# Five instruction orders searched anew, with token parts ahead of raw weights and scatters led by their own copies

## The chip, the cores and the metric

The kernel runs on one core of a Trainium2 chip. Its engines work side by side, each through its own list of instructions: TensorE (PE) multiplies, VectorE (DVE) and ScalarE (ACT) work element by element, GpSimd (POOL) copies and issues indirect DMAs, SyncE (SP) issues the other DMAs. The metric is the device time of one execution in microseconds, the median of several runs.

## The reference

A gated linear recurrence over four sequences of 5056 tokens with 256 channels, and then a mixture of eight experts that sends each token to one expert:

```python
log_a = 8.0 * sigmoid(r_gate) * log(clip(sigmoid(a_param), 1e-6, 1 - 1e-6))
a_t = exp(log_a)
x_gated = sqrt(maximum(1 - a_t * a_t, 1e-6)) * sigmoid(i_gate) * x
h = a_t[:, t] * h + x_gated[:, t]         # for every t; y[:, t] = h
logits = y @ w_gate                        # (20224, 8)
e = argmax(logits, axis=1); gate = softmax(logits)[e]
out[token] = gate * (maximum(y[token] @ w1[e], 0) @ w2[e])    # w1: 256x1024, w2: 1024x256
```

## The kernel before

Tokens are cut into 158 blocks of 128, four blocks to a quad (40 quads, the last one shorter). The front works quad by quad: three loads (r, i, x; `load`, L638), tanh and exp on ScalarE (`th` L647, `ex` L653, `ti` L658), square and square root (`sq` L669, `rt` L675), a product on VectorE (`b` L680) and the recurrence as a scan along the tokens (`scan` L699). TensorE then computes gate logits (`lp` L718, `lt` L733, copied by `ls` and `lg`) and turns the rows token-major (`yt` L756). VectorE takes each row's largest absolute value (`am` L763, `sc`), ScalarE writes the row scaled to float16 (`hi` L783) and VectorE the rest that float16 left over (`lw` L793).

Quads form groups (`GROUPS`). For each group `r1` to `r6` find the expert and the place of every token, with one product on TensorE between (`rk` L830), and the factor `mx`. POOL writes token id and factor behind each row (L786, L879 for the first four quads; L881, L882 for the others, four blocks at once) and scatters the rows block by block into a DRAM buffer sorted by expert (`scat` L888). A fence on SP (`fence` L933) waits for a group's scatters.

The experts work in slots of 256 rows (the last 16 of 128): first layer (`L1` L1129), relu on ScalarE (L1141) and its rest on VectorE (L1149), second layer (`L2` L1169 to L1173), scaled copy out of PSUM (`ot` L1182), and a scatter into the output (`store` L1193). Slots 0 to 7 take the raw float32 weights of experts 0 to 7 (`raw` L1042), one slot each; meanwhile those weights are split into two float16 parts and written back (`wm` L975/L977, `wt` L981, `wh` L995, `wl` L1000, `wr` L1004). Later slots load the split weights (`w` L1057), by a table (`tab`, L1209 on) that says which rows and which expert a slot has.

The first `PICK` = 2 slots don't wait for the buffer: `sel` (L910) makes a 0/1 matrix of the tokens that belong to them, `pick` (L922) multiplies the token rows by it, and `xs` (L928) copies the columns from PSUM, which the first layer then reads. Slots 2 to 7 load their rows from the buffer transposed (`xl` L1080, L1087), and `join` (L1100) adds the two float16 halves on POOL.

The order on every engine comes from a planner that runs before the kernel is built: a list scheduler (`Line`, `Plan`) with a duration, a priority and buffer pools for each task. Priorities are a due time per quad or slot plus an offset per kind (`URGE`). The instructions are then written out in that order and each engine works through its list in order, so an instruction that waits holds up everything behind it on its engine.

## Time and profile before

| | us |
|---|---|
| median of 3 runs (lowest to highest) | 1052.61 (1051.04 to 1054.34) |
| profiled execution | 1058.75 |
| its span, first to last instruction | 1057.0 |
| ScalarE's idle time before its first instruction and before its first data | 0.74 and 0.62 |
| TensorE busy / VectorE / ScalarE / POOL | 989.3 / 676.3 / 619.1 / 435.9 |

The profile comes from one execution, some 6 us above the median. The mean granted TensorE clock is 0.988 of full speed. A window view gives busy time per engine in a stretch; a timeline row gives start, duration, engine, line, operation and tiles, and in square brackets how long the engine sat idle before it and what ended that.

### The profile page before, as it was taken

Reading aid. Unit: us, or ns where it says so; the run is one execution under the profiler, and the core shown is the slowest. Engines: PE = TensorE matmul, PEld = TensorE weight load, DVE = VectorE, ACT = ScalarE, POOL = GpSimd, SP = SyncE. Lnnn points to the kernel's source line nnn. Section 1 sums busy time; section 2 is a strip of 40 time slices with the busy share of each in tenths; the row PEclk is TensorE's granted clock in tenths of the full one; section 3 lists DMA queues with packets and bytes.
Section 4 is the critical chain, followed back from the end, with each engine's and each line's share of the span. In section 5 each row is a group of like instructions: output and inputs, shape, how many; then the busy total and the mean of one; then the engine's idle time right before and its main releaser. Section 6 shows DMA issues by size and latency. Waiting matters only on the chain. (4 is left out here: it accounts for less than half of the span.)

```text
span 1057.0 us, 23781 instructions
## 1 busy us (share of the span) xinstructions
PE 989.3 (94%) x8854; PEld 862.1 (82%) x8854; DVE 676.3 (64%) x1387; ACT 619.1 (59%) x815; POOL 435.9 (41%) x522
## 2 busy tenths in 40 slices
PE   1469899999999999999999999999999999999997
PEld 1138688888888989888888888888888888889987
DVE  4998889887686565876847578466876473232211
ACT  8988685675746467567555765557666442222222
POOL 0264446434555335363452644525264434222222
...
GB/s 367 382 248 209 329 339 314 291 328 369 333 299 290 344 246 342 275 379 203 286 343 356 271 310 269 297 329 302 235 321 295 310 321 140 262 265 326 223 249 26
DMA packets 169347, 307.12 MB, mean 291 GB/s; under 512 B 117636, under 2 KB 122377, under 8 KB 147978
## 3 DMA queue, kind: packets, MB, share of 16 engines
q1 hardware_dynamic: 153770, 262.81, 78.4%
...
## 5 line engine op out<-in xcount | busy, mean ns | idle before, releaser
L1129 PE MATMUL p<-xT,wt 128*128 128x256 f16 (+1 forms) x3936 | 413.6, 263 | 2.5 <-DMA wt<-wscr 2.2
L1129 PEld LDWEIGHTS <-wt 128*128 128x128 f16 x3936 | 354.9, 98 | 40.8 <-DMA wt<-wscr 2.5
L1193 POOL DMA_INDIRECT out<-ot,meta x164 | 181.1, 1104 | 400.2 <-ACT ot L1182 353.7
L1171 PE MATMUL po<-wt,hb 128*128 128x256 f16 x1184 | 322.9, 273 | 8.3 <-ACT ot L1182 6.4
L1149 DVE SCALAR_TENSOR_TENSOR hb<-p,hb 128x1024 f16<-128x1024 f32 x148 | 180.5, 1220 | 224.3 <-ACT hb L1141 207.2
L1173 PE MATMUL po<-wt,hb 128*128 128x256 f16 x1184 | 322.8, 273 | 0.1
L1172 PE MATMUL po<-wt,hb 128*128 128x256 f16 x1184 | 322.8, 273 | 0.1
L1141 ACT ACTIVATE hb<-p 128x1024 f16<-128x1024 f32 (+1 forms) x164 | 167.4, 1021 | 196.7 <-PE p L1129 167.8
L888 POOL DMA_INDIRECT buf<-rows,pi x158 | 172.4, 1091 | 47.8 <-issue 35.8
L1182 ACT ACTIVATE ot<-po,f 128x256 f32<-128x256 f32 x148 | 69.9, 472 | 172.7 <-PE po L1173 125.3
L1172 PEld LDWEIGHTS <-hb 128*128 128x128 f16 x1184 | 115.8, 98 | 21.7 <-issue 8.7
L1171 PEld LDWEIGHTS <-hb 128*128 128x128 f16 x1184 | 115.8, 98 | 16.6 <-issue 2.7
L1173 PEld LDWEIGHTS <-hb 128*128 128x128 f16 x1184 | 115.8, 98 | 13.7 <-issue 0.3
L699 DVE TENSOR_TENSOR_SCAN in_x<-in_r,in_x 128x512 f32<-128x512 f32 (+7 forms) x82 | 97.5, 1198 | 1.4
L680 DVE SCALAR_TENSOR_TENSOR in_x<-in_i,in_x 128x1024 f32<-128x1024 f32 (+1 forms) x38 | 45.7, 1203 | 48.8 <-ACT in_i L675 40.8
L1112 POOL TENSOR_SCALAR f<-meta,wt,wt 128x2 f32<-128x2 f32 (+1 forms) x82 | 37.5, 458 | 95.5 <-DMA wt<-wscr 76.6
L793 DVE SCALAR_TENSOR_TENSOR rows<-yt,fa,rows 128x256 f16<-128x256 f32 x154 | 65.4, 478 | 14.1 <-ACT rows L783 7.1
L783 ACT ACTIVATE rows<-yt,fa 128x256 f16<-128x256 f32 x154 | 61.8, 475 | 7.2 <-DVE fa L775 6.2
L1169 PE MATMUL po<-wt,hb 128*128 128x256 f32 x256 | 62.1, 392 | 1.5 <-ACT ot L1180 1.3
L664 DVE SCALAR_TENSOR_TENSOR in_x<-in_i,in_x 128x1024 f32<-128x1024 f32 (+1 forms) x38 | 46.2, 1221 | 23.5 <-ACT in_i L658 18.5
L1129 PE MATMUL p<-x,wt 128*128 128x256 f32 x256 | 59.3, 386 | 0.7 <-ACT x L928 0.7
L763 DVE TENSOR_REDUCE m<-yt 128x2 f32<-128x512 f32 x77 | 50.2, 678 | 11.2 <-PE yt L756 10.8
...
## 6 DMA issues: line engine op xcount, KB each, us to landing
wt<-wscr SPq DMA_DIRECT2D x164, 1024.5 KB
...
out<-ot,meta POOLq DMA_INDIRECT x164
```

The lines of the kernel that those rows point to most:

```text
L699: V.tensor_tensor_scan(y[:, lo:hi], av[:, lo:hi], y[:, lo:hi], init, ALU.mult, ALU.add)
L793: V.scalar_tensor_tensor(r[:, 2 * p + j, D:2 * D], o["yt", p][:, j], o["sc"][:, 2 * p + j:2 * p + j + 1], r[:, 2 * p + j, 0:D], ALU.mult, ...
L888: i = G.indirect_dma_start(out=buf[:, :], out_offset=bass.IndirectOffsetOnAxis(ap=g["pi"][:, b0 + j:b0 + j + 1], axis=0), in_=rows[q]["row ...
L1129: T.matmul(pv[:, i], wv[:, wl, kk, fs], o["xT"][:, 2 * xl + kk, 0:U], start=(z == 0), stop=(z == len(seq) - 1))
L1141: A.activation(o["h"][:, gs, 0:U] if o["raw"] else o["h"][:, 0, gs, 0:U], o["p1", g], AF.Relu)
L1149: V.scalar_tensor_tensor(o["h"][:, 1, gs, 0:U], o["p1", g], 0.0, o["h"][:, 0, gs, 0:U], ALU.max, ALU.subtract)
L1169: T.matmul(dst, h[:, f, ts], wv[:, f, :], start=(f == 0), stop=(f == NF - 1))
L1171: T.matmul(dst, h[:, 0, f, ts], wv[:, 0, f, :], start=(f == 0), stop=False)
L1172: T.matmul(dst, h[:, 0, f, ts], wv[:, 1, f, :], start=False, stop=False)
L1173: T.matmul(dst, h[:, 1, f, ts], wv[:, 0, f, :], start=False, stop=(f == NF - 1))
L1182: A.activation(o["ot", j], o["po", j], AF.Copy, scale=o["f2"][:, j:j + 1])
L1193: i = G.indirect_dma_start(out=out[:, :], out_offset=bass.IndirectOffsetOnAxis(ap=o["id"][j], axis=0), in_=o["ot", j], in_offset=None, bou ...
```

## The change

The planner gets new durations and group sizes, a priority offset for nearly every single task (the table `NUDGE`, about 1500 entries; one line of it is shown), and a model of how many DMAs may be under way. One slot is picked instead of two. For the first 15 quads (`ROWSUM`) the row's measure is the sum of absolute values, taken on ScalarE by an activation with an accumulator, in place of the largest absolute value on VectorE. The sum of the two halves for raw slots (`join`) moves from POOL to VectorE. For quads that aren't picked, `scat` copies id and factor of its own block before the scatter. The two weight sums under way may use two PSUM columns.

```diff
-GROUPS = (2, 2, 2, 2, 1, 2, 3, 2, 1, 2, 2)
+GROUPS = (1, 3, 2, 2, 1, 2, 1, 2, 1, 1, 2)
 UNITS = 4
-SINGLE = 6
+SINGLE = 2
 BATCH = 2
 PASSES = ((1, 256, 8),)
...
-PICK = 2
-EARLY = 250.0
-ELOAD = 90.0
+PICK = 1
+ROWSUM = 15
+ADDER = 'DVE'
+EARLY = 622.8
+ELOAD = 748
 WIDE = (3,)
...
-URGE = dict(quad=23.0, load=-22.0, norm=-37.0, rows=-11.5, hi=197.0, route=-208.0, scat=335.0, tab=-203.0,
-            first=-850.0, slot=-3250.0, fac=-52.0, store=-90.0)
+URGE = dict(quad=25.2, load=-137.0, norm=-105.3, rows=-55.5, hi=1053.8, route=-211.5, scat=1126.0, tab=-1395.2, first=-482.8, slot=-3722.3, fac=-106.7, store=399.0)
+NUDGE = {
+"L1(0,0)": -59.2, "L1(0,1)": -20, "L1(1,0)": -4, "L1(1,1)": -347.3, "L1(10,0)": 228.2, "L1(10,1)": 2.7,
...
-BUFS = dict(r=3, i=4, x=6, rows=4, yt=2, lp=1, rank=1, tot=1, lg=4, hl=2, xT=4, hb=3, ot=9, po=1, p1=2, reg=3, x32=6)
+BUFS = dict(r=3, i=4, x=6, rows=4, yt=2, lp=1, rank=1, tot=2, inc=4, lg=4, hl=2, xT=4, hb=3, ot=9, po=1, p1=2, reg=3, x32=6)
...
+    LANES = 8
+    DMAS = dict(load=1, raw=1, wr=1, w=1, fence=1, xl=2, blank=2, pads=E)
...
+            if q < ROWSUM:
+                T["am", q, p] = a("ACT", 0.78, pr + URGE["rows"], "am", q, p, after=[T["yt", q, p], T.get(("am", q, 0))], take=[("rows", q)] if p == 0 else [])
+            else:
+                T["am", q, p] = a("DVE", 0.64, pr + URGE["rows"], "am", q, p, after=[T["yt", q, p]])
...
-            T["fa", q] = a("POOL", 0.5, pr + URGE["scat"], "fa", q, after=[T["r6", c], T["hi", q, 0], T.get(("fence", c - 1))] + list(xs),
-                           give=[("lg", c)])
+            if s.picked(q):
+                T["tag", q] = a("POOL", 0.75, pr + URGE["scat"], "tag", q, after=[T["hi", q, 0]])
+            ok = [T["r6", c], T["hi", q, 0], T.get(("fence", c - 1)), T.get(("tag", q))] + list(xs)
+            if s.picked(q):
+                T["fa", q] = a("POOL", 0.65, pr + URGE["scat"], "fa", q, after=ok, give=[("lg", c)])
+                ok = [T["fa", q]]
             for j in range(s.quads[q]):
-                sc.append(a("POOL", 1.27, pr + URGE["scat"], "scat", q, j, after=[T["fa", q], T["lw", q, j // 2]], give=[("rows", q)],
-                            size=0.45))
+                sc.append(a("POOL", 1.28 if s.picked(q) else 1.9, pr + URGE["scat"], "scat", q, j, after=ok + [T["lw", q, j // 2]],
+                            give=[("rows", q)] + ([] if s.picked(q) else [("lg", c)]), size=0.4))
         if g[-1] == s.nq - 1:
             sc = [a("SP", 3.0, -500, "pads", c, after=sc, size=6.0)]
-        T["fence", c] = a("SP", 0.4, -500, "fence", c, after=sc, then=lambda t: s.routed(c))
...
+    def fenced(s, c):
+        s.routed(c)
+        s.add("DVE", 0.01, -1e6, "drop", c, after=[s.tabbed], give=[("inc", c)])
...
-            x = a("POOL", 1.2 * U / 256 + 0.1, -160, "join", k, after=[x], take=[("x32", k)], give=[("xT", k)])
+            if ADDER == "PE":
+                x = T["add", k] = a("PE", 0.5, -98, "add", k, after=[x], take=[("yt", ("x", k))], give=[("xT", k)], slack=SLACK)
+                x = a("ACT", 0.5, -205, "join", k, after=[x], take=[("x32", k)], give=[("yt", ("x", k))])
+            elif ADDER == "DVE":
+                x = a("DVE", 0.1 + 0.5 * U / 256, -205, "join", k, after=[x], take=[("x32", k)], give=[("xT", k)])
+            else:
+                x = a("POOL", 1.2 * U / 256 + 0.1, -160, "join", k, after=[x], take=[("x32", k)], give=[("xT", k)])
...
+    def token_rows(o):
+        if "rows" not in o:
+            o["rows"] = work.tile([P, QB, PITCH], F32, name="rows", bufs=BUFS["rows"])
+        return o["rows"]
+
     @op
     def am(q, p):
         o = rows[q]
-        if p == 0:
+        if "m" not in o:
             o["m"] = small.tile([P, QB], F32, name="m", bufs=4)
-        V.tensor_reduce(o["m"][:, 2 * p:2 * p + 2], o["yt", p], AX.X, ALU.max, apply_absolute_value=True)
+        if q < ROWSUM:
+            r = token_rows(o).bitcast(BF16)
+            for j in range(2 * p, 2 * p + 2):
+                A.activation(r[:, j, 0:D], o["yt", p][:, j % 2], AF.Abs, accum_out=o["m"][:, j:j + 1])
+        else:
+            V.tensor_reduce(o["m"][:, 2 * p:2 * p + 2], o["yt", p], AX.X, ALU.max, apply_absolute_value=True)
 
...
     @op
     def hi(q, p):
         o, nb = rows[q], plan.quads[q]
-        if p == 0:
-            o["rows"] = work.tile([P, QB, PITCH], F32, name="rows", bufs=BUFS["rows"])
+        r = token_rows(o).bitcast(F16)
         for j in range(2):
-            A.activation(o["rows"].bitcast(F16)[:, 2 * p + j, 0:D], o["yt", p][:, j], AF.Copy, scale=o["sc"][:, 2 * p + j:2 * p + j + 1])
-        if p == 0 and plan.group_of[q] <= PASSES[0][0]:
-            for j in range(nb):
-                G.tensor_copy(o["rows"].bitcast(I32)[:, j, D + 1:PITCH], ids[:, q * QB + j:q * QB + j + 1].to_broadcast([P, PITCH - D - 1]))
+            A.activation(r[:, 2 * p + j, 0:D], o["yt", p][:, j], AF.Copy, scale=o["sc"][:, 2 * p + j:2 * p + j + 1])
 
     @op
...
+    def mark(q, j):
+        G.tensor_copy(rows[q]["rows"].bitcast(I32)[:, j, D + 1:PITCH], ids[:, q * QB + j:q * QB + j + 1].to_broadcast([P, PITCH - D - 1]))
+
     @op
     def fa(q):
         g, b0, _ = group(q)
-        r, nb = rows[q]["rows"], plan.quads[q]
-        if plan.group_of[q] <= PASSES[0][0]:
-            for j in range(nb):
-                G.tensor_copy(r[:, j, D:D + 1], g["mx"][:, b0 + j:b0 + j + 1])
-            return
-        G.tensor_copy(r.bitcast(I32)[:, 0:nb, D + 1:PITCH], ids[:, q * QB:q * QB + nb].unsqueeze(2).to_broadcast([P, nb, PITCH - D - 1]))
-        G.tensor_copy(r[:, 0:nb, D:D + 1], g["mx"][:, b0:b0 + nb].unsqueeze(2))
+        for j in range(plan.quads[q]):
+            G.tensor_copy(rows[q]["rows"][:, j, D:D + 1], g["mx"][:, b0 + j:b0 + j + 1])
+
+    @op
+    def tag(q):
+        for j in range(plan.quads[q]):
+            mark(q, j)
 
     @op
     def scat(q, j):
         g, b0, _ = group(q)
         c = plan.group_of[q]
+        if not plan.picked(q):
+            mark(q, j)
+            G.tensor_copy(rows[q]["rows"][:, j, D:D + 1], g["mx"][:, b0 + j:b0 + j + 1])
         i = G.indirect_dma_start(
             out=buf[:, :], out_offset=bass.IndirectOffsetOnAxis(ap=g["pi"][:, b0 + j:b0 + j + 1], axis=0),
             in_=rows[q]["rows"][:, j, :], in_offset=None, bounds_check=E * plan.cap - 1, oob_is_err=False)
...
-            g["sel"] = work.tile([P, 2, NF, 256], F16, name="hb", bufs=BUFS["hb"]).rearrange("p l f u -> p (l f u)")[:, 0:B * PICK * 256]
+            g["sel"] = work.tile([P, 2, NF, 256], F16, name="hb", bufs=BUFS["hb"]).rearrange("p l f u -> p (l f u)")[:, 0:B * PICK * PASSES[0][1]]
...
-                    T.matmul(st["pick"][:, h, 0:PICK * 256], r[:, j, l * D + h * P:l * D + (h + 1) * P], g["sel"][:, b0 + j].rearrange("p k u -> p (k u)"),
+                    T.matmul(st["pick"][:, h, 0:PICK * PASSES[0][1]], r[:, j, l * D + h * P:l * D + (h + 1) * P], g["sel"][:, b0 + j].rearrange("p k u -> p (k u)"),
...
     def join(k):
 
         o = slots[k]
-        U = o["U"]
         x = work.tile([P, 2, 256], F32, name="x32", bufs=BUFS["x32"])
-        G.tensor_tensor(x[:, :, 0:U], o["xT"][:, 0:2, 0:U], o["xT"][:, 2:4, 0:U], ALU.add)
+        if ADDER == "PE":
+            A.copy(x, o["xT"])
+        else:
+            U = o["U"]
+            (V if ADDER == "DVE" else G).tensor_tensor(x[:, :, 0:U], o["xT"][:, 0:2, 0:U], o["xT"][:, 2:4, 0:U], ALU.add)
         o["xT"] = x
...
     def wt(e, i):
-        T.matmul(misc[:, 508:509], ones32, prepared[e, i]["m"], start=True, stop=True)
+        o = prepared[e, i]
+        staged(o)
+        z = 508 + next(sums) % BUFS["tot"]
+        o["tot"] = misc[:, z:z + 1]
```

Three places of the written order follow, the first on SP: the start of the queue of loads, behind the loads of constants. `in_r`, `in_i`, `in_x` and `hb` are tiles for the gates and tokens of a quad, `wt` tiles for raw weights, 1 MB each (a load of 128x1024 is 0.52 MB). Before:

```order
L1042 DMA wt12_141<-in_w 128x2048
L1042 DMA wt02_138<-in_w 128x2048
L638 DMA in_r_147<-in_rix 128x1024
L638 DMA in_i_149<-in_rix 128x1024
L638 DMA in_x_151<-in_rix 128x1024
L1042 DMA wt11_140<-in_w 128x2048
L1042 DMA wt01_137<-in_w 128x2048
L1042 DMA wt10_139<-in_w 128x2048
L1042 DMA wt00_136<-in_w 128x2048
L638 DMA hb_158<-in_rix 128x1024 x2
L638 DMA in_x_162<-in_rix 128x1024
L638 DMA hb_165<-in_rix 128x1024 x2
```

And now (`hb_95` has gates of the third quad, `hb_155` of the fourth; `buf_80` is the buffer, which is filled with padding rows):

```order
L1134 DMA in_i_149<-in_rix 128x1024
L1134 DMA in_x_151<-in_rix 128x1024
L1134 DMA in_i_153<-in_rix 128x1024
L1134 DMA hb_155<-in_rix 128x1024
L1134 DMA in_x_157<-in_rix 128x1024
L1134 DMA hb_155<-in_rix 128x1024
L1134 DMA in_r_164<-in_rix 128x1024
L1560 DMA wt00_138<-in_w 128x2048
L1134 DMA hb_95<-in_rix 128x1024
L1560 DMA wt01_139<-in_w 128x2048
L1831 DMA buf_80<-pad_129 256x1x272 x2
L1134 DMA in_x_186<-in_rix 128x1024
```

Six raw weights stood ahead of the token parts (`in_x_162`, later `in_x_168`) of the third and fourth quad; now two raw weights are queued by the time that all four quads have their parts, the last at `in_x_186`.

The second place is ScalarE's queue in front of the copy `xs` (`x32_678` before, `x32_641` now), which hands the picked columns to slot 0. L975 and L1485 are `wm`, L995 and L1509 `wh`, L783 and L1288 `hi`, L675 and L1171 `rt`. The 12 rows that end with it, before:

```order
L975 ACTIVATE hl_553,wm_552<-wt11_140 128x2048
L849 ACTIVATE lg_495<-lg_495 128x64
L653 ACTIVATE in_r_231<-in_r_231,k4_89 128x1024
L975 ACTIVATE hl_573,wm_572<-wt01_137 128x2048
L669 ACTIVATE in_i_190<-in_r_231 128x1024
L675 ACT_TABLE_LOAD
L675 ACTIVATE in_i_185<-in_i_185,quarter_103 128x1024
L995 ACTIVATE hl_553<-wt11_140,wsc_631 128x2048
L675 ACTIVATE in_i_190<-in_i_190,quarter_103 128x1024
L658 ACT_TABLE_LOAD
L658 ACTIVATE in_i_204<-in_i_204 128x1024
L928 COPY x32_678<-p1_383 128x512
```

Now, rows of the new order that end 11 ahead of that copy (L1267 is the new row reduction `am`):

```order
L1509 ACTIVATE hl_348<-wt01_139,wsc_389 128x2048
L1485 ACTIVATE hl_411,wm_410<-wt00_138 128x2048
L1267 ACTIVATE rows_435,m_434<-yt_404 128x256 x2
L1221 COPY ls_441<-misc_133 128x128
L1267 ACTIVATE rows_435,m_434<-yt_429 128x256 x2
L1267 ACTIVATE rows_457,m_456<-p1_443 128x256 x4
L1288 ACTIVATE rows_435<-yt_404,fa_350 128x256 x2
L1351 ACTIVATE lg_315<-lg_315 128x96
L1288 ACTIVATE rows_435<-yt_429,fa_350 128x256 x2
L1149 ACTIVATE in_r_164<-in_r_164,k4_89 128x1024
L1288 ACTIVATE rows_457<-p1_443,fa_350 128x256 x4
L1154 ACTIVATE in_i_265<-in_i_265 128x1024
```

Before, two of the four sums of weights (L975) and one of the three scaled parts (L995) stood directly ahead of the copy, with two table loads. Now row reductions (L1267) stand between the sums of weights and the row copies (L1288), and of the sums of weights only two are left ahead of the copy.

The third place is POOL, from the last picked quads on: L879 and L1382 copy factors, L786 and L1376 ids, L888 and L1397 scatter, L1100 is the sum `join`, L1188 and L1717 scale, L1193 and L1722 store. Before (rows of the last two picked quads, `rows_506` and `rows_519`):

```order
L879 COPY rows_506<-mx_545 128x1 x4
L888 DMA buf_80<-rows_506,pi_568 166400x272 x4
L879 COPY rows_519<-mx_545 128x1 x4
L888 DMA buf_80<-rows_519,pi_568 166400x272 x4
L1100 ISA
L1100 TENSOR_TENSOR x32_799<-xT_742 128x512
L1100 TENSOR_TENSOR x32_821<-xT_757 128x512
L1100 TENSOR_TENSOR x32_852<-xT_777 128x512
L1188 TENSOR_SCALAR ot_854<-ot_854,meta_733 128x256
L1100 TENSOR_TENSOR x32_862<-xT_784 128x512
L1193 DMA out_0<-ot_854,meta_733 20224x256
```

And now, without the numbers of the tiles:

```order
L1376 COPY rows<-ids 128x15 x8
L1382 COPY rows<-mx 128x1 x12
L1397 DMA buf<-rows,pi 166400x272 x12
L1722 DMA out<-ot,meta 20224x256
L1717 ISA
L1717 TENSOR_SCALAR ot<-ot,meta 128x256 x2
L1722 DMA out<-ot,meta 20224x256 x3
L1376 COPY rows<-ids 128x15
L1396 COPY rows<-mx 128x1
L1397 DMA buf<-rows,pi 166400x272
```

The sums of two halves are gone from POOL. The factors of the last three picked quads stand together in front of their 12 scatters, which slot 1 now waits for. From the fourth group on, each scatter has its own copy of id and factor in front, where one pair of copies (L881, L882) led four scatters.

## Rows read from the trace of the kernel before

**Rows 1.** The page: busy time, share and instructions of each engine.

```profile
PE 989.3 (94%) x8854; PEld 862.1 (82%) x8854; DVE 676.3 (64%) x1387; ACT 619.1 (59%) x815; POOL 435.9 (41%) x522
```

**Rows 2.** Windows: start:end, length; busy time (x count) of PE, PEld, DVE, ACT, POOL; PEclk; DMA share; GB/s.

```profile
0.00:79.79 79.79, 32.97 (x176) 16.57 (x176) 61.18 (x153) 71.38 (x84) 26.41 (x49) 0.91 0.89 334
10.00:30.00 20.00, 4.49 (x29) 3.19 (x29) 10.94 (x20) 19.12 (x22) 0.92 (x5) 1.00 1.01 418
80.42:104.35 23.93, 23.93 (x130) 20.38 (x131) 20.77 (x33) 22.00 (x24) 10.13 (x9) 1.00 0.74 197
104.35:131.30 26.95, 22.84 (x111) 17.94 (x110) 22.35 (x25) 17.23 (x20) 12.64 (x10) 0.91 1.04 324
131.30:1052.30 921.00, 909.53 (x8441) 807.18 (x8439) 571.37 (x1179) 507.34 (x686) 385.13 (x455) 1.00 0.92 290
```

**Rows 3.** Groups by line, ACT, 0 to 79.79: count, busy us, mean ns, idle before.

```profile
L975 ACT ACTIVATE hl<-wt 128x2048 bf16<-128x2048 f32 x4 | 7.6, 1909 | 0.0
L675 ACT ACT_TABLE_LOAD x5 | 6.4, 1283 | 0.1
L995 ACT ACTIVATE hl<-wt,wsc 128x2048 f16<-128x2048 f32 x3 | 5.9, 1987 | 0.0
...
L975 ACT ACTIVATION_READ_ACCUMULATOR hl<-wt 128x1 f32 x4 | 0.8, 201 | 0.0
```

**Rows 4.** Timeline of ACT: start us, duration us, engine, line; [idle before, releaser].

```profile
21.55 1.56 ACT L783 ACTIVATE rows<-yt,fa 128x256 f16<-128x256 f32 x4
...
79.79 1.07 ACT L928 COPY x<-p 128x512 f32<-128x512 f32 x2 [0.89 <-PE p L922]
```

**Rows 5.** Timeline of PE around the first slots and at slot 8.

```profile
80.42 3.72 PE L1129 MATMUL p<-x,wt 128*128 128x256 f32 x16 [0.67 <-ACT x L928]
...
88.40 1.07 PE L718 MATMUL misc<-in_x,wg 128*32 128x256 f32 x16
...
92.96 0.38 PE L733 MATMUL misc<-cst,ls 128*128 128x128 f32 x2
93.18 0.28 PE L981 MATMUL misc<-wm,ones 128*128 128x1 f32 x2
93.32 3.70 PE L1169 MATMUL po<-wt,hb 128*128 128x256 f32 x16
96.86 0.60 PE L756 MATMUL yt<-cst,in_x 128*128 128x128 f32 x4
...
205.14 2.78 PE L1129 MATMUL p<-xT,wt 128*128 128x256 f16 x24
```

**Rows 6.** Timeline of POOL: scatters, first sum, the fourth group.

```profile
51.65 2.80 POOL L879 COPY rows<-mx 128x1 f32<-128x1 f32 x4
...
69.40 0.72 POOL L879 COPY rows<-mx 128x1 f32<-128x1 f32 x4 [6.91 <-DVE mx L871]
...
75.69 3.91 POOL L879 COPY rows<-mx 128x1 f32<-128x1 f32 x4
...
84.58 0.97 POOL L888 DMA_INDIRECT buf<-rows,pi  x1 [0.30 <-issue]
96.06 1.16 POOL L1100 TENSOR_TENSOR x<-xT 128x512 f32<-128x512 f16 x1 [10.51 <-DMA xT<-buf]
...
143.99 0.98 POOL L1193 DMA_INDIRECT out<-ot,meta  x1 [10.84 <-DMA in_i<-in_rix]
```

**Rows 7.** L879 by itself: min, median, max in ns.

```profile
L879 POOL COPY rows<-mx x16: 176/258/2246, 45.3 to 78.4; 128x1 f32<-128x1 f32 x16
```

**Rows 8.** Groups by line, POOL, whole span.

```profile
L879 POOL COPY rows<-mx 128x1 f32<-128x1 f32 x16 | 8.1, 555 | 41.2 <-DVE mx L871 41.2
...
L786 POOL COPY rows<-ids 128x15 int32<-128x15 int32 x16 | 4.5, 326 | 8.2 <-DMA ids<-in_ids 8.2
```

**Rows 9.** Timeline of SP's queue: the fences at L933.

```profile
90.84 0.25 SPq L933 DMA_DIRECT2D fence<-buf  x1
...
183.42 0.26 SPq L933 DMA_DIRECT2D fence<-buf  x1
```

More of the change, by code (lines that the diff above doesn't have):

```diff
@@ L180, in run @@
                         continue
+                    if e == "POOL" and k.size and now < s.clear(e) - 1e-9:
+                        continue
                     p = (k.prio + (SWITCH if k.table and k.table != s.act else 0), k.seq)
@@ L206, in run @@
                     k.end = s.dma + 1.2
+                    if k.name == "xl" and k.size > 1:
+                        d = max(d, s.dma - 0.5 - now)
+                        s.free[e] = now + d
+                        heappush(s.events, (now + d, next(s.ids), None))
                 else:
                     k.end = now + d
+                n = 1 if e == "POOL" and k.size else 0 if e != "SP" else 1 if k.name == "xl" and k.args[0] < PICK else s.DMAS.get(k.name, 0)
+                if n:
+                    s.lanes[e] += [k.end if k.size else now + 2.0] * n
+                    z = s.clear(e)
+                    if z > now + d:
+                        if e == "SP":
+                            s.free[e] = z
+                        heappush(s.events, (z, next(s.ids), None))
                 heappush(s.events, (k.end, next(s.ids), k))
@@ L370, in route @@
+        T["r3", c] = a("DVE", 0.58 * f, pr, "r3", c, after=[T["rk", c]], take=[("inc", c)], give=[("rank", c)])
+        T["r4", c] = a("DVE", 0.2 * f, pr, "r4", c, after=[T["r3", c]])
+        T["gt", c] = a("ACT", 0.2 * f, pr - 6, "gt", c, after=[T["r1", c]], table="T")
+        T["r5", c] = a("DVE", (0.45 if c <= PASSES[0][0] else 0.3) * f, pr, "r5", c, after=[T["r4", c]])
+        T["r6", c] = a("DVE", 0.7 * f, pr, "r6", c, after=[T["gt", c], T["r5", c]] + [T["sc", q] for q in g])
         sc = []
@@ L481, in slot @@
         assert not near or raw
-        x = T["xl", k] = a("SP", 0.5 if near else 1.7, p0 + (0.3 if head else 0.1), "xl", k, after=[reg], take=[] if near else [("xT", k)], give=gr,
+        x = T["xl", k] = a("SP", 0.5 if near else 1.95, p0 + (0.3 if head else 0.1), "xl", k, after=[reg], take=[] if near else [("xT", k)], give=gr,
                            size=0.2 if near else 1.9 * U / 256)
@@ L506, in slot @@
         more = o.get("more")
-        fac = None if near else a("POOL", 0.44, URGE["fac"], "fac", k, after=[x] + w)
+        fac = None if near else a("POOL", 0.32, URGE["fac"], "fac", k, after=[x] + w)
         if near:
@@ L1094, in join, with add, weights @@
     @op
+    def add(k):
+        o = slots[k]
+        x, o["xT"] = o["xT"], ps_y.tile([P, 2, D], F32, name="yt")
+        for l in range(2):
+            T.matmul(o["xT"], id16, x[:, 2 * l:2 * l + 2], start=(l == 0), stop=(l == 1))
+    @op
     def join(k):
         o = slots[k]
-        U = o["U"]
         x = work.tile([P, 2, 256], F32, name="x32", bufs=BUFS["x32"])
-        G.tensor_tensor(x[:, :, 0:U], o["xT"][:, 0:2, 0:U], o["xT"][:, 2:4, 0:U], ALU.add)
+        if ADDER == "PE":
+            A.copy(x, o["xT"])
+        else:
+            U = o["U"]
+            (V if ADDER == "DVE" else G).tensor_tensor(x[:, :, 0:U], o["xT"][:, 0:2, 0:U], o["xT"][:, 2:4, 0:U], ALU.add)
         o["xT"] = x
+    def weights(o, i):
+        return o.get("head", o)["w", i]
     @op
```

230 lines of the change are left out of this document (125 added, 105 removed), and 438 rows, old and new, of the table NUDGE.

## The prediction, on record before the result

> **What bounds the kernel now.** I read the windows first, because one share of 94% for TensorE [rows 1] hides two different halves. Up to the first matmul of an expert, at 80.42 us [rows 5], TensorE is busy 33.0 us of 79.8, while ScalarE is busy 71.4 [rows 2]. From then on TensorE loses nothing until 104.35, 4.1 us between 104.35 and 131.30, and 11.5 us between 131.30 and 1052.30 (921.00 less 909.53) [rows 2]. Behind 1052.30 come 4.7 us of the last store. So the end is the start of the first expert matmul, plus a chain of TensorE work, plus some 15.6 us of holes, plus that tail. The chain of work is the same in both kernels: 90 slots, the same two layers, the same transposes. What can move is the start of the chain, and the holes.
>
> What holds the start back is read from ScalarE's timeline: the copy that hands the picked columns to slot 0 starts at 79.79, the first matmul follows at 80.42 [rows 4, 5]. ScalarE was idle only 8.4 us before it [rows 2], 1.4 of them before its first data. So ScalarE's own queue is what to count.
>
> **The change part by part.** *Loads.* In the DMA queue the last token part of the four picked quads (of four 128-token blocks each) stood behind 6 MB of raw weights; now 2 MB of raw weights stand ahead of it. With everything else that is 12.9 MB up to that part before and 9.8 now (0.52 a part, 1.05 a weight), and at the 0.418 MB/us of 10 to 30 us [rows 2] it lands 7.4 us earlier. That is a permission; the gain is what ScalarE makes of it.
>
> *ScalarE in front of the first expert matmul.* Counted in the two orders, from ScalarE's first tanh to that copy:
> - table loads 11 before, 6 now: 5 x 1.283 = 6.4 us less [rows 3];
> - sums of absolute weights 4 before, 2 now: 2 x 1.9 = 3.8 less; scaled weights 3 before, 2 now: 2.0 less [rows 3];
> - one square root fewer and one tanh more, of one shape: taken as nothing;
> - 16 activations more, which take the row reductions over from VectorE. No such form stands in the trace. Nearest is the activation that writes the same 128x256 from the same PSUM tile, four in 1.56 us, 0.39 each [rows 4]. The accumulator is read by an instruction of 0.20 [rows 3], which in the weights' sums lies almost wholly beside the next activation. So 0.39 to 0.59; I take 0.45, near the lower end: 7.2 us more (6.2 to 9.4).
> Sum: -5.0 us (-6.0 to -2.8).
> [...]
>
> *ScalarE's idle time there*: 7.0 us behind the first 1.4, in waits for VectorE and TensorE. VectorE loses eight row reductions in this stretch, and the data are in earlier. Walking the new order with the durations above, ScalarE finds its inputs ready almost everywhere, at three places by under 1 us; I take half of that time as gone, 3.5 us (0 to 7.0). The picks are half as wide (256 columns for one slot, not 512 for two); by the same walk they end some 3 us before ScalarE reaches the copy, so this brings nothing more.
> **First expert matmul: 80.4 - 5.0 - 3.5 = 71.9 us** (67.4 to 77.6).
>
> *The handover to slot 1.* Slot 1 was picked too; now it comes through memory like slots 2 to 7: factors, scatters, fence, transposing load, sum of two halves. The factors of the last picked group are ready near 58 us (they follow the copy of its last gate logits by some 6 us in both orders). POOL then copies 12 factor columns at 0.555 us, the mean [rows 8], 6.7 us (2.1 by the shortest [rows 7], 11.7 by the slowest four, which took 3.91 [rows 6]), and issues 12 scatters at 0.97 + 0.30 [rows 6], 15.2: the last ends near 80. Before, the fence went out 5.3 us after the last scatter ended (85.55 to 90.84), and the first sum began 5.2 after the fence (96.06) [rows 6, 9], 1.0 of it spent on two small loads that no longer stand there. So the sum begins near 89.7 and ends near 90.5; it runs on VectorE now, not on POOL at 1.16 [rows 6].
> TensorE is through slot 0 after four half-layers of 3.54 from start to start (93.32 to 96.86) and 2.4 of transposes, gate projection and small ones [rows 5]: 16.6 us, at 88.5. Slot 1 waits 2.0 us (0 to 7, if the copies take the long form), and all of TensorE's queue waits behind it.
> ScalarE has 15.3 us of other work between its second and third relu here; by my count the third and the fourth come 0.7 and 0.5 us late. Two weight sums fall behind the first expert matmul that stood ahead of it, 0.3 [rows 5]. Together **+3.5**.
>
> *The old holes between 104 and 131*, 4.1 us [rows 2], wait for outputs of slots 0 and 1, for low halves of token rows, and for a bank shared by weight sums and ranks. VectorE no longer does the row maxima here and POOL no longer the sums. I take 3 as gone (0 to 4.1): **-3**.
>
> *From 131 us on*: 11.5 us of holes [rows 2]. An order does not tell which copy out of PSUM will be late. Bounds: all gone, or nearly as much again. I take 2 as gone: **-2** (-9 to +9). The row reductions of 15 of the 40 quads sit on ScalarE, 44 activations more at 0.45, 20 us; ScalarE is busy 507 of 921 us there [rows 2], which covers them.
>
> *The scatters of all other rows* get an id copy and a factor copy in front of each, 142 of them, in place of one pair for four blocks. With 0.326 for the id copy and 0.555 for the factor [rows 8] that is about 125 us, less some 20 for the pairs, on a POOL that is busy 385 of 921 [rows 2]. Nothing on TensorE follows POOL closely there except the first table (the last rival). Cost taken: 0.
>
> **Sum**: -8.5 + 3.5 - 3 - 2 = -10.0 us. The profiled execution took 1058.75 us, 1.75 beyond its span, so 1048.75 by this sum; the median shown, 1052.61, is 6.1 below the profiled one, and the same difference gives **1042.6 us**.
>
> **The rivals.** *The order also closes the later holes.* ScalarE's idle time is gone and the reductions cost 0.41 (first matmul at 67.9, -12.5), +3.5 at the handover, no hole from 104 to 131 (-4.1), and a third of the 11.5 stays (-7.7): -20.8, **1032 us**. For it: nothing but order makes those holes, no engine but TensorE is full behind 131. Against it: ScalarE's thin margins.
>
> *The start is gained and lost again.* The reductions cost 0.59 and the idle time stays: first matmul at 77.6, slot 1 ready by then. ScalarE, busy 22.0 of 23.9 us between 80.42 and 104.35 [rows 2], gets eight reductions more at such a place; relus come late until about 130 and give the 2.8 back: **1052 us**. For it: ScalarE's share there. Against it: with two PSUM banks TensorE bears a half-layer of lag.
>
> *Slower, by POOL.* The copies in front of every scatter run long, and the fence behind the fourth group, which must pass before the first table of slots, comes late. Place: 16 blocks before 183 us. Before, that fence went out at 183.42 [rows 9] and slot 8's first matmul ran at 205.14 [rows 5]; table, loads and weights between need some 14 us, so about 8 were to spare. POOL stood idle 10.84 us in one piece just before its first scatter there [rows 6]. A factor copy of x us adds 16 x (x + 0.3) us; that eats idle piece and slack from x = 0.85 on. At 1.4 slot 8 is 8 us late and the end hangs on it: **1059 us**; the longest copy, 2.246 [rows 7], would make it 22. For it: four copies took 0.72 us at one place and 2.80 at another [rows 6]. Against it: the mean is 0.555, and in the new TensorE order the transposes of both groups stand 20 us and more earlier by count.
> [...]
>
> **How the numbers follow.** Forecast 1042.6, its own range 1036 to 1048: 0.52. Later holes closed, 1032: 0.21. Gained and lost, 1052: 0.18. POOL, 1059: 0.09. A measurement of this kernel can tell 0.3%, 3.2 us, from no change: faster is below 1049.5, slower above 1055.8. Faster are the first two and about a quarter of the third: 0.78. Slower are POOL's case and a little of the third: 0.10. The same: 0.12. The range, 1031 to 1053, leaves out POOL's case and about half of the second case's lower part.
>
> **What would show each step.** First expert matmul near 72, with six table loads and 16 new activations of 0.4 to 0.5 each on ScalarE before it; at 78 or later the first step is wrong. Slot 1's first matmul waits 0 to 7 us, for the sum on VectorE; more means POOL's path was mispriced. TensorE's holes: about 1 us from there to 131 beside late relus, about 9.5 behind; above 20 the forecast is wrong whatever the start did. Factor copies on POOL of 0.2 to 0.6 us on average; at 0.85 or more POOL's case is on.

## The result, and the profile after

The changed kernel takes 1067.9 us (median of 4, 1065.31 to 1069.76) against 1052.7 (1051.04 to 1054.34): ratio 1.0143, 95% interval 1.0114 to 1.0171. It is slower by 1.4%, where 1042.6 was forecast. Its profiled execution took 1066.82 us, its span 1065.0. The engines' totals, as in [rows 1], look as before, though ScalarE and POOL have more to do:

```profile
PE 988.4 (93%) x8856; PEld 864.4 (81%) x8856; DVE 659.5 (62%) x1380; ACT 632.0 (59%) x931; POOL 471.4 (44%) x726
```

The same windows as in [rows 2] (start:end, length; busy time of PE, PEld, DVE, ACT, POOL; PEclk; DMA share; GB/s), cut at the new first expert matmul:

```profile
0.00:66.05 66.05, 24.37 (x172) 17.71 (x172) 47.48 (x125) 64.13 (x105) 19.96 (x46) 0.89 0.94 363
66.67:104.35 37.68, 37.21 (x182) 31.53 (x183) 32.48 (x45) 33.17 (x52) 12.41 (x10) 0.93 0.70 185
104.35:131.30 26.95, 25.80 (x142) 21.72 (x141) 17.67 (x38) 22.72 (x41) 11.70 (x16) 1.00 0.97 303
131.30:240.00 108.70, 95.88 (x567) 80.77 (x566) 82.23 (x166) 74.94 (x112) 57.93 (x80) 0.94 0.94 312
240.00:1060.30 820.30, 804.88 (x7798) 712.71 (x7797) 479.13 (x1008) 435.95 (x621) 367.81 (x576) 1.00 0.94 293
```

TensorE starts on the experts at 66.67, 13.75 us before [rows 5], and loses 1.6 us until 131.30. Then it loses 12.8 us by 240 (108.70 less 95.88) and 15.4 behind. TensorE's timeline names the large holes (start, duration, line, tiles; in brackets the idle time ahead and what ended it):

```profile
66.67 6.27 PE L1658 MATMUL p<-x,wt 128*128 128x256 f32 x16 [4.17 <-ACT x L1438]
...
86.31 4.05 PE L1658 MATMUL p<-x,wt 128*128 128x256 f32 x18
...
141.38 6.44 PE L1658 MATMUL p<-x,wt 128*128 128x256 f32 x16 [3.19 <-DMA wt<-in_w]
...
186.35 0.44 PE L1229 MATMUL misc<-cst,ls 128*128 128x128 f32 x2 [2.29 <-DVE hl L1502]
...
233.89 5.30 PE L1658 MATMUL p<-xT,wt 128*128 128x256 f16 x24 [3.91 <-DMA wt<-wscr]
```

The start waits for ScalarE's copy, as forecast. Slot 1 waits for nothing (86.31). Slot 5 waits 3.19 us for its raw weights, a transpose at 186 waits 2.29 us for VectorE (L1502, a step of the weights' splitting, which reads `misc`, the PSUM tile that the transpose writes, and had itself waited 0.64 us for a write-back), and slot 10 waits 3.91 us for split weights. Three of these rows are also long: 16 matmuls took 6.27 and 6.44 us where such a row took 3.72 before [rows 5], and 24 took 5.30 in place of 2.78. Windows over just these rows show why (PEclk is the third column from the end):

```profile
66.67:72.90 6.23, 6.23 (x18) 5.09 (x19) 6.16 (x6) 6.20 (x6) 5.05 (x4) 0.58 0.64 220
141.38:147.66 6.28, 6.28 (x16) 5.04 (x17) 6.25 (x7) 2.00 (x1) 5.72 (x7) 0.56 0.96 369
233.89:239.10 5.21, 5.21 (x25) 3.71 (x26) 0.00 (x0) 0.00 (x0) 1.53 (x4) 0.50 1.02 345
```

The granted clock was 0.58, 0.56 and 0.50 in the mean of the three stretches (0.50 from 66.67 to 68.00 and from 141.38 to 143.00, 1.00 again from 72.00 and from 147.66 on), each time behind a hole of 3.2 to 4.2 us. The three rows cost 2.55 + 2.72 + 2.52 = 7.8 us beside the holes. On SP's queue the loads for slot 5 look like this (the engine's time is the issue alone):

```profile
78.10 0.25 SPq L1443 DMA_DIRECT2D fence<-buf  x1
...
106.92 8.58 SPq L1603 DMA_TRANSPOSE xT<-buf  x1
...
123.27 0.33 SPq L1560 DMA_DIRECT2D wt<-in_w  x1
123.64 0.43 SPq L1518 DMA_DIRECT2D wscr<-hl  x1
127.61 1.42 SPq L1560 DMA_DIRECT2D wt<-in_w  x2
129.08 0.45 SPq L1518 DMA_DIRECT2D wscr<-hl  x1
```

The fence that frees slot 1 goes out at 78.10. A transposing load then stands 8.58 us in the queue at 106.92. Three loads of raw weights (L1560, one at 123.27, two at 127.61) and two write-backs of split weights (L1518), of 1.05 MB each, go out between 123.27 and 129.5, and PE gets slot 5's weights at 141.38. At the 303 GB/s of the window up to 131.30 these 5.24 MB alone take 17.3 us, to 140.6; that fits, but whose bytes went first the rows don't tell.

### The profile page after: what moved, and what is told of

Its sections match the earlier page's. It is cut to its first block, busy times and chain, and to the rows that moved or that the text cites. A ratio compares the mean times of both kernels' runs of the same rounds, so it can differ in the third digit from the quotient of the medians.

```text
span 1065.0 us, 24108 instructions
## 1 busy us (share of the span) xinstructions
PE 988.4 (93%) x8856; PEld 864.4 (81%) x8856; DVE 659.5 (62%) x1380; ACT 632.0 (59%) x931; POOL 471.4 (44%) x726
## 5 line engine op out<-in xcount | busy, mean ns | idle before, releaser
L1722 POOL DMA_INDIRECT out<-ot,meta x164 | 176.2, 1074 | 393.4 <-ACT ot L1711 354.5
L1397 POOL DMA_INDIRECT buf<-rows,pi x158 | 176.9, 1120 | 57.2 <-POOL rows L1396 40.6
L1195 DVE TENSOR_TENSOR_SCAN in_x<-in_r,in_x 128x512 f32<-128x512 f32 (+5 forms) x82 | 95.0, 1178 | 1.3
L1288 ACT ACTIVATE rows<-yt,fa 128x256 f16<-128x256 f32 x154 | 62.3, 478 | 24.4 <-DVE fa L1281 17.9
L1252 PE MATMUL yt<-cst,in_x 128*128 128x128 f32 x308 | 46.7, 287 | 27.2 <-DVE in_x L1195 22.3
L1658 PE MATMUL p<-x,wt 128*128 128x256 f32 x256 | 63.2, 405 | 7.8 <-ACT x L1438 4.2
L1176 DVE SCALAR_TENSOR_TENSOR in_x<-in_i,in_x 128x1024 f32<-128x1024 f32 (+1 forms) x38 | 45.6, 1202 | 31.8 <-ACT in_i L1171 31.8
L1658 PEld LDWEIGHTS p<-x,wt 128*128 128x128 f32 x256 | 51.8, 205 | 16.3 <-ACT x L1438 4.5
```

Source lines behind the costliest of these rows:

```text
L1195: V.tensor_tensor_scan(y[:, lo:hi], av[:, lo:hi], y[:, lo:hi], init, ALU.mult, ALU.add)
L1288: A.activation(r[:, 2 * p + j, 0:D], o["yt", p][:, j], AF.Copy, scale=o["sc"][:, 2 * p + j:2 * p + j + 1])
L1397: i = G.indirect_dma_start(out=buf[:, :], out_offset=bass.IndirectOffsetOnAxis(ap=g["pi"][:, b0 + j:b0 + j + 1], axis=0), in_=rows[q]["row ...
L1658: T.matmul(pv[:, i], wv[:, wl, kk, fs], o["xT"][:, 2 * xl + kk, 0:U], start=(z == 0), stop=(z == len(seq) - 1))
L1722: i = G.indirect_dma_start(out=out[:, :], out_offset=bass.IndirectOffsetOnAxis(ap=o["id"][j], axis=0), in_=o["ot", j], in_offset=None, bou ...
```

## The experiments

All are the changed kernel with one edit, or the kernel before where that is said; edits are shown shortened. Ratios are to the kernel before on the same chip; its median there was 1053.0 to 1054.6 us, so ratios tell more than medians. Four theories. **A**: the splitting of raw weights (sum, scale, two halves, write-back) comes too late by its place in the queues or by its work, and holds the buffers of the next raw loads. **B**: DMA transfers set the pace from 96 us on, so that an earlier start only runs into them. **C**: the row sums make ScalarE's copies and relus late. **D**: POOL's copies make fences late.

**A second trace of the kernel before** (no edit).

> The kernel before, unchanged, traced a second time, because its first profiled execution (1058.75 us) lies 6 us above its median. If that execution was one of the usual ones with some late places in it, the second trace has a span near 1051, the first expert matmul again near 80.4, and lacks some of the holes of the first (2.18 us at 318 and 1027). If instead profiling always costs this kernel 6 us, the span is 1057 again.

Measured: 1051.89 us, span 1050.0. Its windows from its first expert matmul on:

```profile
79.30:131.30 52.00, 48.88 (x252) 40.53 (x253) 43.77 (x61) 41.86 (x47) 27.20 (x18) 0.97 0.89 267
131.30:240.00 108.70, 107.96 (x682) 93.80 (x681) 96.66 (x186) 78.57 (x96) 55.14 (x57) 1.00 0.97 328
240.00:1045.30 805.30, 797.41 (x7747) 709.53 (x7745) 473.50 (x991) 426.07 (x588) 327.69 (x399) 1.00 0.92 287
```

It starts at 79.3, has 11.75 us of holes, and the hole of 2.18 us at 1027 is gone (the one at 314 is not). So the first profiled execution was a long one by 7.0 us, and the honest comparison is with this trace: span +15.0 = start -12.65, holes +18.1 (29.86 less 11.75), the same matmuls longer by +9.5 (963.77 less 954.25; 7.8 of it the three rows above).

**Row maxima on VectorE again (e2), copies in pairs again (e3).**

```diff
-        if q < ROWSUM:                       # e2, in am and sc; order unchanged
+        if q < 0:
-        if not plan.picked(q):               # e3, in scat
-            mark(q, j)
+        if not plan.picked(q) and "led" not in rows[q]:
+            ... ids and factors of the quad's four blocks, two instructions
```

> The changed kernel with its written order, but the row measure of all quads is again the largest absolute value, taken on VectorE (30 reductions of two blocks in place of 60 activations on ScalarE, each at the place in the sequence where the activations stood). Theory C (the activations on ScalarE make copies out of PSUM and relus late): 8 to 15 us faster than the changed kernel, 1053 to 1060. Theory A (the splitting of raw weights comes late): ScalarE has about 24 us less to do, but what holds the splitting is its place in the queues, so -3 to +3, 1065 to 1071. Theory B (DMAs are full from 96 to 250 us): within 2 us.

> The changed kernel with its written order, but ids and factors of a quad that isn't picked are again copied by one pair of instructions for its four blocks, in front of its first scatter. Theory D (POOL's copies make fences late, so table and transposed rows come late): 5 to 12 us faster, 1056 to 1063. Theories A, B and C: within 2 us of the changed kernel, 1066 to 1070.

Measured: e2 1070.16 us, 1.0191 (1.0150 to 1.0232); e3 1073.85, 1.0207 (1.0178 to 1.0236). Neither part undone gives anything back, so C and D don't hold in this order; the pairs are slower, with an interval just clear of the changed kernel's (up to 1.0171).

**Splitting moved up (e4), with its write-backs (e6), with less to reduce (e5).**

```diff
+EARLIER = wm(1,1), wm(2,0) before relu(2,1); wt, ws, wh, wl behind them; raw(4,1), raw(5,0) ahead   # e4
+EARLIER = wr(0,1), wr(2,1), raw(3,1) before raw(4,0); then as e4, and wr(1,1), wr(2,0)              # e6
-            V.tensor_reduce(o["m"], o["w"], AX.X, ALU.max, ...)                                     # e5, ScalarE's sum alike
+            V.tensor_reduce(o["m"], o["w"][:, 0:F // 2], AX.X, ALU.max, ...)
```

> The changed kernel with 12 instructions of its order moved up: for two raw weights (w2 of expert 1, w1 of expert 2) the sum of absolute values goes ahead of a relu for which ScalarE waited 4.16 us at 102.7, and the steps behind it follow some 7 us earlier; the raw loads of expert 4's w2 and expert 5's w1, which wait for the buffers of these, are issued near 116 and 120 in place of 123.3 and 128. Theory A (the splitting is late, and holds the buffers for the next raw loads): TensorE's hole of 3.19 us at 141 and the 6.44 us matmuls at half clock behind it go, 3 to 6 us faster, 1062 to 1065. Theory B (DMAs are full there): the load lands near 141 whenever it is issued, within 2 us of 1067.9. Theories C and D: no change.

> The changed kernel with 17 instructions moved up. In the run before this one with moved sums (e4) ScalarE stood 7.0 and 2.7 us on write-backs issued at 98.9 and 100.5, since these hold the two staging buffers. Here both write-backs and one raw load go out near 86 to 88, where DMAs are busy 0.26 to 0.46, and then the two weights' steps as in e4, with their write-backs and the raw loads that follow. Theory A as order: no wait on write-backs at 102, no hole at 141 (3.19 us and the half clock behind it, 2.7): 4 to 8 us faster than the changed kernel, 1060 to 1064. Theory B (DMAs are full from 96 on, however early a load is issued): within 2 us.

> The changed kernel, order unchanged; of 12 of the 16 raw weights (those after the first four) only a quarter of the columns goes into the measure that sets their scale, which leaves out three quarters of that reduction: 1.7 us less on VectorE (8 times) or 1.4 on ScalarE (4 times), some 19 us of engine time between 99 and 195 us. If the splitting is late because ScalarE and VectorE have too much to do there (theory A, as work): the last low half ends 8 us or more before 226 and the kernel is 4 to 8 us faster, 1060 to 1064. If it is late by its place in the queues and by the write-backs that hold the two staging buffers (theory A, as order): within 3 us of 1067.9. Theory B (DMAs): within 2 us.

Measured: e4 1071.91 us, 1.0184 (1.0154 to 1.0215). The hole at 141 is gone, but ScalarE's moved sums now wait for write-backs, and TensorE for ScalarE:

```profile
109.26 1.91 ACT L1486 ACTIVATE hl<-wt 128x2048 bf16<-128x2048 f32 x1 [7.03 <-DMA wscr<-hl]
...
113.95 1.91 ACT L1486 ACTIVATE hl<-wt 128x2048 bf16<-128x2048 f32 x1 [2.69 <-DMA wscr<-hl]
```

```profile
118.64 0.47 PE L1230 MATMUL misc<-cst,ls 128*128 128x128 f32 x1 [8.30 <-ACT ls L1222]
```

e6: 1071.58 us, 1.0136 (1.0083 to 1.0190). No wait on write-backs, no hole of slot 5; a new one on an output copy instead, and slot 10 waits longer:

```profile
148.13 3.12 PE L1699 MATMUL po<-wt,hb 128*128 128x256 f32 x8 [2.94 <-ACT ot L1712]
...
237.96 4.26 PE L1659 MATMUL p<-xT,wt 128*128 128x256 f16 x24 [4.41 <-DMA wt<-wscr]
```

e5: 1066.69 us, 1.0112 (1.0079 to 1.0144). The last low half ends 4.4 us earlier (224.4 against 228.8), not 8 or more. Slot 10 starts 4.5 us earlier than in the changed kernel and still waits 3.8 for its weights; by 488 the lead is gone in another wait for a load:

```profile
229.37 4.08 PE L1661 MATMUL p<-xT,wt 128*128 128x256 f16 x24 [3.79 <-DMA wt<-wscr]
...
487.99 7.19 PE L1661 MATMUL p<-xT,wt 128*128 128x256 f16 x49 [2.50 <-DMA wt<-wscr]
```

Theory A is not the cause by itself: moved or shortened, the splitting only changes what is waited for next.

**Holes filled (e7), and e6 with the first hole filled (e8).**

```diff
+        for i in range({(0, 0): 10, (5, 0): 8, (10, 0): 10}.get((k, g), 0)):    # e7, in L1; e8 slot 0 alone
+            T.matmul(pv[:, i % n], cst[:, 0:P], cst[:, 0:U], start=True, stop=True)
```

> The changed kernel, order unchanged, with 10, 8 and 10 matmuls on constants (128x256 float32, 0.38 us each) in front of the first layers of slots 0, 5 and 10, into the bank that these overwrite. They stand in the holes of 4.17, 3.19 and 3.91 us and end about when the awaited data come. If the half clock behind these holes costs what the rows say (16 matmuls in 6.27 and 6.44 us in place of 3.70, 24 in 5.30 in place of 2.78), and is lost time: 5 to 8 us faster, 1060 to 1063, and those rows read 3.7, 3.7 and 2.8. If the time is lost anyway to data that come later still: within 2 us.

> The moves of e6_prep and the 10 matmuls on constants in front of slot 0 alone. If both causes are real and add up: 2 to 3 us below e6_prep; if the early lead is always given back in the stage of the raw slots: equal to e6_prep.

Measured: e7 1069.33 us, 1.0122 (1.0066 to 1.0178). The rows are short (16 matmuls in 3.72 us at 66.70 and in 3.62 at 142.29, 24 in 2.78 at 232.76, where the changed kernel took 6.27, 6.44 and 5.30), and the time comes back as waits behind them, such as 2.81 us on an output copy at 262, where the changed kernel waits 0.50:

```profile
138.75 3.70 PE L1657 MATMUL p<-cst 128*128 128x256 f32 x16
142.29 3.62 PE L1661 MATMUL p<-x,wt 128*128 128x256 f32 x16
...
261.95 0.27 PE L1703 MATMUL po<-wt,hb 128*128 128x256 f16 x1 [2.81 <-ACT ot L1714]
```

e8: 1079.26 us, 1.0211 (1.0156 to 1.0266); its interval overlaps that of e6 (up to 1.0190), and why its middle is higher was not followed. So no gain from filling the holes is seen, and in the trace of e7 the 7.8 us come back as waits (slot 13 starts at 274.45 against 275.81, the span is 1066.9 against 1065.0). The interval of e7 is wide: it does not rule out a gain of 5 us.

**Half the bytes of split weights: in the changed kernel (e9), in the kernel before (e10).**

```diff
-        nc.sync.dma_start(wscr[e, i], prepared[e, i]["t"])
+        nc.sync.dma_start(wscr[e, i][:, 0:2 * F + 2], prepared[e, i]["t"][:, 0:2 * F + 2])
-            nc.sync.dma_start(t, wscr[o["e"], i])           # and the load with a register
+            nc.sync.dma_start(t[:, 0:2 * F + 2], wscr[o["e"], i][:, 0:2 * F + 2])
-                T.matmul(pv[:, i], wv[:, wl, kk, fs], ...   # L2 alike
+                T.matmul(pv[:, i], wv[:, 0, kk, fs], ...
```

> The changed kernel, order and TensorE's work unchanged, but only the high halves of the split weights are written back and loaded (0.5 MB each in place of 1), and the low halves' matmuls read the high halves again: this leaves the low halves of the weights out of the result. 16 write-backs and 164 loads: some 92 MB less of 314. Theory B (DMAs set the pace from 96 us on): the holes at 141, 234, 488 and 721 go, the lead of the start stays, 1040 to 1050. Theory A (the place of the splitting in the queues): the holes at 141, 186 and 234 stay within 1.5 us each, 1060 to 1068.

> The same in the kernel before: high halves alone are written back and loaded, the low halves left out of the result. It has few holes that wait for DMAs (0.9 and 0.6 near 256 to 268, 2.2 at 1027 in one of two traces): 1046 to 1052 by both theories. With it the two orders stand side by side where DMAs have room: the changed one ahead by 6 us or more if DMAs took its lead, behind if its order did.

Measured: e9 1051.28 us, 0.9970 (0.9949 to 0.9990); e10 1047.49, 0.9945 (0.9925 to 0.9965). The same order, the same work of TensorE, and 18 us less (1.0143 to 0.9970), where the kernel before gains 6. Theory A's range for e9 (1060 to 1068) is ruled out; theory B's (1040 to 1050) is missed by 1.3 us. By the sign set for e10, the changed order, now not ahead in spite of its early start, lost part of its lead in itself. The rows of e9 that answer to those of the changed kernel above:

```profile
66.82 6.46 PE L1658 MATMUL p<-x,wt 128*128 128x256 f32 x16 [4.15 <-ACT x L1438]
...
140.02 3.69 PE L1658 MATMUL p<-x,wt 128*128 128x256 f32 x16 [1.47 <-DMA wt<-in_w]
...
180.09 0.44 PE L1229 MATMUL misc<-cst,ls 128*128 128x128 f32 x2 [0.59 <-DVE hl L1502]
...
223.10 2.78 PE L1658 MATMUL p<-xT,wt 128*128 128x256 f16 x24
```

The wait of slot 10 is gone, that of slot 5 is 1.47 and no longer followed by a low clock (1.00 from 131.30 to 250.00; 3.69 us for the row, not 6.44), that at 180 is 0.59. The row at 66.82 is slow as before: it waits for a copy, not for a transfer. DMA share and rate (last two columns) in two stretches, first the changed kernel, then e9:

```profile
96.00:131.00 35.00, 33.69 (x177) 28.63 (x177) 25.69 (x49) 27.13 (x55) 16.43 (x19) 1.00 1.01 297
196.00:240.00 44.00, 37.92 (x289) 31.42 (x288) 29.95 (x80) 26.67 (x47) 24.03 (x34) 0.92 0.99 316
```

```profile
96.00:131.00 35.00, 33.68 (x179) 28.48 (x178) 25.88 (x49) 27.12 (x55) 15.64 (x19) 1.00 0.91 267
196.00:240.00 44.00, 42.12 (x368) 36.60 (x367) 29.64 (x75) 29.60 (x51) 25.36 (x41) 1.00 0.87 269
```

The starts of some slots (first matmul of the first layer, from the timelines) show where the lead goes:

| slot | before, 2nd trace | changed | e10 (before, light) | e9 (changed, light) |
|---|---|---|---|---|
| 0 | 79.32 | 66.67 | 78.51 | 66.82 |
| 4 | 139.30 | 127.48 | 140.19 | 127.83 |
| 5 | 154.79 | 141.38 | 155.68 | 140.02 |
| 8 | 201.44 | 197.96 | 202.29 | 191.70 |
| 10 | 230.74 | 233.89 | 231.58 | 223.10 |
| 13 | 269.66 | 275.81 | 269.78 | 262.05 |
| 89 | 1033.06 | 1051.73 | 1031.97 | 1037.12 |

Slots 0 to 4 of the changed order start alike with full and with half transfers (0.4 us apart). Between slots 4 and 13 full transfers cost it 14 us, and hardly more behind (13.8 at slot 13, 14.6 at slot 89). The kernel before starts slot 13 at 269.7 with either. That is theory B, shown by taking the transfers away, for this stretch; e9 halves write-backs and loads together, and which of them counts was not separated.

Behind slot 13 it is something else. Windows from slot 13's start to 4.7 us before the end of the span, where little but the last store is left; one row each for the table's four columns, in their order:

```profile
269.66:1045.30 775.64, 770.27 (x7496) 686.10 (x7493) 449.22 (x934) 408.76 (x562) 317.01 (x387) 1.00 0.91 284
275.81:1060.30 784.49, 770.62 (x7485) 683.28 (x7483) 454.74 (x961) 414.84 (x578) 345.37 (x544) 1.00 0.93 293
269.78:1044.20 774.42, 768.53 (x7496) 685.22 (x7493) 449.94 (x934) 409.10 (x562) 323.76 (x387) 1.00 0.69 199
262.05:1045.70 783.65, 770.54 (x7485) 683.77 (x7483) 456.13 (x962) 415.62 (x580) 347.20 (x544) 1.00 0.72 206
```

TensorE is busy alike, but the changed order takes 8.9 us more there with full transfers and 9.2 more with half: its holes are 13.9 and 13.1 us, those of the kernel before 5.4 and 5.9. So the 15.0 us of span are -12.65 at the start, +18.8 up to slot 13 (4.0 with half transfers) and +8.9 behind, which is there with half the bytes of split weights as well.

**One part alone in the kernel before: copies for each scatter (b1), row sums on ScalarE (b2).**

```diff
+            ... ids and factor of block j in front of its scatter; the pair in fa gone          # b1
-        V.tensor_reduce(o["m"][:, 2 * p:2 * p + 2], o["yt", p], AX.X, ALU.max, ...)           # b2, for q < 15
+            A.activation(rows[:, j, 0:D], o["yt", p][:, j % 2], AF.Abs, accum_out=o["m"][:, j:j + 1])
```

> The kernel before with its own order, and one part of the change alone: each unpicked scatter led by its own copy of id and factor. Undoing this in the changed kernel (e3) made it some 6 us slower. If such copies suit the chip by themselves (the first scatter of a quad leaves sooner): 2 to 6 us faster than the kernel before. If they only fit the order that was searched with them: within 2 us. Theory D (they make fences late): 5 us slower or more.

> The kernel before with its own order, and one part alone: the row measure of the first 15 quads is the sum of absolute values on ScalarE. ScalarE has 60 activations more, 0.37 us and 0.20 for the read of the sum beside the next one; 16 of them stand before the first expert matmul: 6 us later there by 0.36 each, less what VectorE's eight reductions held up. Theory C: 5 to 10 us slower, the later 44 costing too. Theories A and B: 3 to 6 us slower, and nothing behind 130 us.

Measured: b1 1053.31 us, 0.9993 (0.9972 to 1.0014): no change. b2 1061.81 us, 1.0098 (1.0068 to 1.0129). Windows up to the copy for slot 0, the second trace of before and b2:

```profile
0.00:78.70 78.70, 30.50 (x176) 15.93 (x176) 60.07 (x152) 71.52 (x84) 26.32 (x49) 0.93 0.89 335
```

```profile
0.00:82.60 82.60, 30.46 (x176) 16.06 (x176) 54.80 (x144) 76.81 (x116) 25.24 (x49) 0.92 0.85 319
```

That copy comes 3.9 us later, with 5.3 us more on ScalarE (76.81 busy against 71.52); the rest comes later. So in an order not made for them the row sums do cost 8 us by the medians, 10 by the ratio, as theory C had it; in the changed order taking them away gave nothing.

**Later loads out of the way (e11), idle DMA time used (e12).**

```diff
+EARLIER = the five loads of quads 10 and 11 behind the third fence                # e11
+EARLIER = as e11; wr(0,1), wr(2,1), raw(3,1) before raw(4,0)                       # e12
```

> The changed kernel with one thing moved: the five loads of gates and tokens for quads 10 and 11, which SP issues at 129.6 to 135.3, right behind the raw load for slot 5 (issued near 128.5, landed 141.4), go behind the fence of the third group, near 146; ScalarE needs them at 152 or later. Theory B, as sharing (what is issued behind a transfer takes its bandwidth): the raw load lands 2 us or more earlier, the hole of 3.19 us and the half clock behind it go, the kernel is 3 to 6 us faster, 1062 to 1065. Theory B, as a queue (what was issued ahead must be through first): the raw load lands near 141 again, within 2 us; or slower, since the loads now meet the next write-backs.

> As e11_later, and two write-backs and one raw load, issued at 99 to 101 in the changed kernel, go out near 86 to 88, where DMAs were busy 0.26 to 0.46; nothing moves on the other engines, unlike in e6. If free DMA time is what the order lacks: the transposing load that stood 8.6 us in SP's queue from 106.9 goes at once, what follows is issued some 3 us earlier, and the kernel is 1 to 4 us below e11_later. If not: equal to it.

Measured: e11 1067.78 us, 1.0141 (1.0086 to 1.0196); e12 1068.28, 1.0138 (1.0080 to 1.0195). In e11 slot 5 starts 0.7 us earlier, still behind a hole and with a long first row (5.30 us, where e9 has 3.69), and slot 10 waits 4.09 us for split weights, as in the changed kernel (3.91):

```profile
140.65 5.30 PE L1659 MATMUL p<-x,wt 128*128 128x256 f32 x16 [2.22 <-ACT hb L1671]
```

The bracket names a relu on ScalarE, but that isn't what slot 5 waits for: in e9 the same matmuls start at 140.02, while that relu still runs.

```profile
139.69 1.01 ACT L1670 ACTIVATE hb<-p 128x1024 f32<-128x1024 f32 x1
```

So it is the load again, less than 1 us earlier, where sharing was to give 2 or more: the loads behind take little of slot 5's bandwidth, and what is ahead of it is left as the explanation. In e12 slot 5 starts at 142.13, later than in the changed kernel: a few transfers moved into idle time don't help. Which transfer of 96 to 240 us is one too many was not found. No version that is faster than both came out.

## Why the prediction was wrong

| step | forecast | measured, against the first trace of before |
|---|---|---|
| first expert matmul | -8.5 | -13.75 |
| wait of slot 1 | +3.5 | none |
| holes between the start and 131 | -3 | -2.5 |
| holes behind 131 | -2 (-9 to +9) | +16.8 |
| the same matmuls, longer | not in the sum | +7.5 |
| from the profiled execution to the median | -6.1 | +1.1 |

*The start* was right in mechanism and too small in size. ScalarE did 7.2 us less before its copy (64.13 busy against 71.38) and stood idle 1.9 us against 8.4. The 16 sums run 0.36 us from start to start, with their reads beside the next one, not 0.45:

```profile
23.92 0.36 ACT L1267 ACTIVATE rows<-yt 128x256 bf16<-128x256 f32 x1
24.18 0.19 ACT L1267 ACTIVATION_READ_ACCUMULATOR rows<-yt 128x1 f32 x1
24.27 0.37 ACT L1267 ACTIVATE rows<-yt 128x256 bf16<-128x256 f32 x1
...
66.05 0.56 ACT L1438 COPY x<-p 128x512 f32<-128x512 f32 x1
```

Six table loads came, as counted. *The handover* was priced too high: the factors came at 54.5, not 58, the 12 factor copies took 2.81 us, the fence went at 78.10, and the sum on VectorE began at 84.93, 4.8 before the forecast:

```profile
54.50 2.81 POOL L1382 COPY rows<-mx 128x1 f32<-128x1 f32 x12 [3.10 <-DVE mx L1373]
```

That slot 1 did not wait at all was luck in part: TensorE took 19.6 us over slot 0 and what lies behind it (66.67 to 86.31), not the 16.6 of the forecast, 2.55 of it with the granted clock at 0.58; after 16.6 us it would have waited 2.3 for that sum.

*The step that failed* is "From 131 us on". I took 2 us of its holes as gone, and my upper bound was nearly as much again; they came to 28.2 us, beyond the 20 that were to show the forecast wrong. Two things had no price in it, the transfers up to slot 13 and the new order's own waits behind it. I had read [rows 2] for ScalarE and POOL, which have room there, and not for transfers, whose share stood at 1.04 from 104 to 131 and at 0.92 behind in the same rows. A chain that starts 8 us earlier asks for its raw and split weights 8 us earlier; I let transfers only permit the start and never asked who pays for the lead. With half the bytes of split weights slot 13 starts 13.8 us earlier in the changed order and no earlier in the kernel before. Behind two of the holes the granted clock was 0.56 and 0.50, which cost 2.72 and 2.52 us, another term that my sum did not have. Behind slot 13 the order has 8.5 us of holes more than the kernel before with full transfers and 7.2 with half; an order does not tell its late copies, as I wrote, and my middle value took them as fewer.

The last row of the table is a second, smaller error: 6.1 us were the distance of one long execution from its median, and I carried them over to another kernel.

*The rivals.* Later holes closed: they grew. Gained and lost again: right in its shape by luck, since the loss was put on ScalarE's relus before 130. POOL: wrong. Its factor copies took 0.27 us in the mean, as forecast, far below the 0.85 from which that case was to start, and in the order of before b1 shows them free:

```profile
L1396 POOL COPY rows<-mx 128x1 f32<-128x1 f32 x142 | 37.8, 266 | 14.4 <-DVE mx L1373 13.5 <-DVE lg L1238 0.8
```

What the order itself loses behind slot 13 (the windows under e9 and e10) stands mostly before output copies. TensorE waits for one 19 times there in the changed kernel, 17 times in e9, 4 times in the second trace of before (waits: total us, times, longest), in that order:

```profile
PE po L1700 <- ACT ot L1711: 9.8, 19, 1.2
PE po L1700 <- ACT ot L1711: 10.0, 17, 1.2
PE po L1171 <- ACT ot L1182: 4.0, 4, 2.2
```

That these come from where second layers follow each other directly in the new order was not tried.
